# Key-feature sums of layer B through two additions on GpSimd, and a new table of order

## The chip, the cores and the metric

The kernel runs on one core of one Trainium2 chip. The metric is the device time of one execution in microseconds, as the median over several runs. Five engines work side by side, each through its own list of instructions in order: PE (TensorE, matrix products into PSUM), ACT (ScalarE), DVE (VectorE), POOL (GpSimd) and SP (SyncE, which here issues nearly all DMAs). They wait for one another by semaphores only.

## What is computed

Two layers A and B alternate, twice, on 2048 tokens of 512 features with 32 heads of 16. A is attention inside four segments of 512 tokens plus a memory of the earlier segments; B is linear attention whose features are softmaxes over the 16 features of a head. All arrays are bf16. Cut to what matters here:

```python
# A, for each segment s
logits = einsum('bhqd,bhkd->bhqk', qs, ks) * scale + mask
a_dot = einsum('bhqk,bhkd->bhqd', softmax(logits), vs)
a_mem = (phi(qs) @ M) / (phi(qs) @ z + 1e-6)
o = g * a_mem + (1 - g) * a_dot
# B
pk = einsum('bhsd,hdf->bhsf', k, w_phi)
phi_k = concatenate([softmax(pk, -1), softmax(-pk, -1)], -1)
kv = einsum('bhsf,bhsd->bhfd', phi_k, v)
z = einsum('bhsf->bhf', phi_k)
o = einsum('bhqf,bhfd->bhqd', phi_q, kv) / (einsum('bhqf,bhf->bhq', phi_q, z) + 1e-6)
# the block, done twice with the same weights
x = x + A(layernorm(x));  x = x + B(layernorm(x))
```

The softmaxes of B need, for each token, head and sign, the sum over 16 exponentials. These sums over the key features are what the change is about.

## The kernel before

The program first records every operation as a node of a graph, with what it reads, writes and which engines could do it (`Graph.op`, L130; an entry such as `{"dve": (262.0, fn)}` gives the engine, a planned duration in ns and the code). Nothing in the program orders these nodes by itself: `ORDER`, a compressed text at the end of the file, holds one list over all operations, the engine of each, and the buffer of each tile. `place` (L157) reads it, and `emit` (L190) writes each engine's instructions in the order of the list, with a semaphore wait wherever an operand, or a buffer that is used again, comes from another engine. So two things set when an instruction can start: its place in its engine's list, and its waits. The planned durations have no effect on the chip.

Buffers come from pools: `pQ` (6 key-mask tiles), `pK` (6 query tiles), `p1` and `p2` (16 and 19 general tiles of 512 and 1024 bf16 elements, both shown as `p` in the profile), `pE`, `pF` (exponentials of the diagonal blocks), `pT`, `pV`, `pW` (values), `pS` (small f32 tiles), and `pD`, four PSUM tiles of 1024 f32 (shown as `D`).

`setup` (L450) loads the inputs, makes the constants on GpSimd and DVE (identity, head pattern, the triangle `tri` and `two64` that add the mask through a matmul), scales the value weights WA_v by the gates (L530, on GpSimd) and clears parts of the pools.

For each segment, `ln` (L574) does the layer norm: statistics on DVE (L577, L578), the reciprocal root on GpSimd (L585, L587; on ACT for the first four tiles) and the scaling on DVE (L594, L598), then a transposition by DMA (L364) or PE. `a_proj` (L658) projects keys and queries of a group g of 8 heads into one PSUM tile. The keys are copied out by ACT or DVE (`Kev`, by `evac`, L358 to L360), and four masks per group (L679, label `Km`, tile `pQ`) each copy them with all heads but some set to zero, so that one matmul makes the logits of several heads: 4 groups x 4 segments x 2 layers x 4 = 128 instructions of 128x512, all on DVE. `phi` (L629) makes the memory's features (L634, L635).

`a_att` (L768) makes the logits on PE from masks and queries (labels `S`, `Sf`, `Sd`, the matmuls of L326 that read `pQ`), ACT takes the exponential out of PSUM (L351), and PE multiplies with the values (L326, `pV` and `pW`). DVE divides (L846, L847) and adds the memory part (L851). `out_proj` (L877) adds to X (L898 on DVE, or a copy by ACT or DVE where PE adds X itself).

`b_keys` (L922) takes one or two token tiles at a time. PE projects them (`BK`), ACT makes the exponentials of both signs (`kexp`, 1024 elements for two tiles), DVE sums each run of 16 (L945), takes the reciprocal (L389, tile `pT`) and multiplies it into the values straight out of PSUM (L973), and PE multiplies with the exponentials (`KV`, L341 with `pT`); DVE accumulates (L911). Per layer there are seven units of two tiles and two of one, so 28 sums of 1024 elements and 8 of 512 in all. `b_query` (L987) does the queries.

Of the kernel before, what the change touches and what calls it, by code (L numbers as in the profile page):

```python
# [17 lines left out]
H = 32  # L18
# [279 lines left out]
class Kernel:  # L298
# [16 lines left out]
    def sb(self, name, shape, dt):  # L315
        return self.es.enter_context(self.nc.sbuf_tensor(name, shape, dt))
# [79 lines left out]
    def alloc(self):  # L396
# [9 lines left out]
        self.two64 = sb("two64", [128, 2, 64], BF16)  # L406
        self.tri = sb("tri", [128, 64], BF16)
# [42 lines left out]
    def setup(self):  # L450
# [39 lines left out]
        for g in range(NG):  # L490
            for hf in range(2):
# [16 lines left out]
        v(lambda e: e.tensor_tensor(self.two64[:], self.ident[:, 0:64][:, None, :].to_broadcast([128, 2, 64]),  # L508
                                    self.ident[:, 64:128][:, None, :].to_broadcast([128, 2, 64]), ALU.add), 120, [R("ident")], [R("two64")])
        tw = self.T(self.p1, "fold")  # L510
        v(lambda e: e.memset(tw.t[:, 0:128], -1e9), 150, [], [tw], eng=P)
        v(lambda e: e.affine_select(tw.t[:, 0:128], tw.t[:, 0:128], [[-1, 128]], ALU.is_gt, 0.0, base=0, channel_multiplier=1), 250, [tw], [tw], eng=P)
        for hf in range(2):
            v(lambda e, hf=hf: e.tensor_copy(self.tri[64 * hf:64 * hf + 64, :], tw.t[64 * hf:64 * hf + 64, 64 * hf:64 * hf + 64]), 100,
              [tw], [R("tri", hf)])
# [142 lines left out]
    def a_proj(self, L, s):  # L658
# [7 lines left out]
        for g in range(NG):  # L666
# [11 lines left out]
            for sl in range(4):  # L678
                fn = lambda e, KM=KM, KT=KT, sl=sl: e.tensor_scalar(  # L679
                    KM.t[:, :, sl % 2, :, 64 * (sl // 2):64 * (sl // 2) + 64], KT.t[:].rearrange("p (j h k) -> p j h k", j=4, h=2),  # L680
                    self.m4[:, sl:sl + 1], None, op0=ALU.mult)
                self.g.op({"dve": (262.0, fn)}, [KT, R("m4")], [KM[sl]], label="Km", port=True)
# [85 lines left out]
    def a_att(self, L, s, i0):  # L768
# [7 lines left out]
        oT = self.oT[("a", L, s * 4 + i0)] = self.T(self.p2, "oT")  # L776
        two = lambda hf: self.two64[64 * hf:64 * hf + 64].rearrange("p a b -> p (a b)")
        tri = lambda hf, n: self.tri[64 * hf:64 * hf + 64, None, :].to_broadcast([64, n, 64])
        trir = [R("two64"), R("tri", 0), R("tri", 1)]
        for gg in range(2):  # L780
            PV = self.T(self.pD, "pv")
            for g in (2 * gg, 2 * gg + 1):
# [5 lines left out]
                for j in range(i0 + 1):  # L788
                    for p in range(2):
# [6 lines left out]
                        else:  # L796
                            P = PF[p] = self.T(self.pF, "PF")
                            self.mm(lambda S=S, j=j, p=p, key=key, qry=qry: [
                                (S.t[:, hf * 512 + 256 - 192 * x:hf * 512 + 512 - 256 * x], key(hf, j, p, x), qry(hf, 64 * x, 256 - 64 * x), x == 0, False)
                                for x in range(2) for hf in range(2)] + [  # L800
                                (S.t[:, hf * 512 + 64:hf * 512 + 448].rearrange("p (b c) -> p b c", b=2)[:, :, 0:64], two(hf), tri(hf, 2), False, True) for hf in range(2)],
                                [], rd + trir, [S], opens=[P], label="Sf", rows=64, dur=252)
                            self.act(lambda P=P: P.t[:, :, 64:512], lambda S=S: S.t[:].rearrange("p (a b) -> p a b", a=2)[:, :, 64:512], ACT.Exp, 896, [S], [P],
                                     scale=0.25, label="expf")
                S = self.T(self.pD, "S")
                PE = self.T(self.pE, "PE")
                self.mm(lambda S=S, key=key, qry=qry: [
                    (S.t[:, hf * 512 + p * 192 + 64 * (1 - x):hf * 512 + p * 192 + 192 - 128 * x], key(hf, i0 + 1, p, x), qry(hf, 128 + 64 * x, 128 - 64 * x), p + x == 0, False)
                    for p in range(2) for x in range(2) for hf in range(2)] + [
                    (S.t[:, hf * 512:hf * 512 + 384].rearrange("p (a b) -> p a b", a=2)[:, :, 0:128], two(hf), tri(hf, 4), False, True) for hf in range(2)],  # L810
                    [], rd + trir, [S], opens=[PE], label="Sd", rows=64, dur=286)
                self.act(lambda PE=PE: PE.t[:, :, 64:256], lambda S=S: S.t[:, :].rearrange("p (a b) -> p a b", a=2)[:, :, 0:384].rearrange("p a (c e) -> p a c e", c=2),
                         ACT.Exp, 768, [S], [PE], scale=0.25, label="expd")

# [107 lines left out]
    def b_keys(self, L, c, parts):  # L922
# [4 lines left out]
        for part in parts:  # L927
            Es, Vts = {}, {}
            units = [part[i:i + 2] for i in range(0, len(part), 2)]
            for u in units:  # L930
# [9 lines left out]
                for sgn in range(2):  # L940
# [3 lines left out]
                             ACT.Exp, 512 * n, [S[0], S[512]][:n], [E[sgn]], scale=1.0 - 2.0 * sgn, label="kexp")  # L944
                    fn = lambda e, sgn=sgn, eo=eo, Z=Z, n=n: e.tensor_reduce(Z.t[:, 0:64 * n].rearrange("p (k s h) -> p k s h", k=n, s=2)[:, :, sgn, :],  # L945
# [177 lines left out]
COPIED = {(L, t) for L in range(2) for t in range(16)}  # L1123
N_WARM = 26
# [5 lines left out]
c-rlH1GFW}vTa60y4Ggfwr$(CZQHhO+qP}nw(ag$wYu*)=lb4<KmHrz)!wTzvnn%k=8PGUReP@_tTL;@;<M;1F{{d|vFfY_tI2Ay+N=(%%j&WEtO0At8nMQ#32Vxlv  # L1130
F5A=Ysp%%)~pR{%i6K_tOJX~G>gk(u$U|s14ay4QRc9GtQdR3^0PAR5-Y$8vf?ZmE5ypOa;!Wn!5HIAF~NdZWM)}*_LSvdIaw}Nl2u^2*=6>OMPtud0(OO6W$9T)R+
trGrC4%SnpI?ZSYB3%^<y_!3U-qvV)s}=cAvdqx7cm=fIVcHSZbDrrDJJXR+fcjW`<>8ci1)7k@aVt*Z|g<4P|{<5B7+SVv>bncUdqCVUJk^HjoWrgV<o!ouy>)SQj
>$jbUTia2NrT*bFujX0lN*opoj1SWniA&0<SfR4M{RVLn^RIzty&#=61^)(r|lVOYslvEHmF3}egLY&L<-W5ZcAn#20AFOZPNvAOIzd&#0OAKS&&u+=OQ+spQ_P!^W
;0tUGtH)MnC0FVQ6!Yej{4TaYX!GTn4BuhkJ0dN8P$`tru7<7lVY#n>U*0Ub)jeTUvAP?k+d{6-LLP3}a$zc+#fwfQ^N<uLx0sWyb3;+%v7=c0!?;r(~f`zO!B&YZA
mQ7~wSw9#LDPc5hfC(@LQo%+T0%Kt+OoMSSp2cRVAq9PB8`wMci6QoeJ}?;8!6LRE5>pad%m_73VI04~2bjnN8vG6xKf)%M0+V4LPGth7vCU8x2Ej%)AIm{S*u(-LH
aWPN4TR}nU<Q0<)uB8jWpQW=+sPzUg6L2KDnM<RgE62E%*Cou4QfIys0;OA9#nz(&;aT~We8vqSs>fZ%78>4W@DcqCM1G*kQib?LudqzVH+%iee4k14$EN)B!T_xFp
CedVLM9-OJNr5fFPI+J7Ez7!yH%)bD;?=fTpkl_CNyo0Y6v>M27GX1;Rm8hycwXEktFXAsk~E5dt9;62eS4#?rtSwgDHyMqCM7;0RlVTVXZsg<04ZBEeDC9Kt{g2nz
>TJBS7c*&198yJ0r2#hO?Pcfl&y2m2uow1>FV5;{ODNJ;T1E_8&gtTk+7wQ(KR!Sz@an_@Gpgq3jy7Q;5s2@ZgT;<$s&#A_H84`Efjj#cn5R>x>q4I5$&oQ46|2oGQ
&M#ngq0H<RRCd7jn79(OLyZ|k*IX1?N&;$=ceQb#hur9X3dbj`&K{yP-Fc^&SDLlr)nAjTI;9-b?r{D;jhD&e-7UB}@i-mA0_QOTk5ewsDEP|=%3`D215QEM^TRaM#
@CYu$m3RzS;8Dy3Jux#J$766DVq+Fqj=eA)^v3ki8Bah42*s<A2s1)b>VsXdKMuh5*Z~J(cN~P9um^U<E!Yh=<2KxZ=iwv_#vz!R;^I(@NtfX|T!X}TlC{HOSQ3*_8  # L1140
amFl;x0UacVIi7#J#kS?!rBI06TFvX2vUc6|-Pg+=F{D9-hL}I2>=_2#iGuXdmv!5_li-VGbOL1uz>vgqwH<Z@^j1h57Lk-oyKN6Yk(;yo*V2C+(u7m<(^jEl7`%@e
yRioR}L^Vpezz889_oz(@EPZ{ZWTjjL%5J%#7+40h8VdWb9OJf6c&^Z+m7Dr!NUsU^LJ4)g|6;1hg`X)rs!h2)qCCtxa^hy^hUcBJLBf@;!QYDKl^DXpW{^o-I{7wS
ssC=1o5^fU@HP(x}&S*a)Wpk~yLn$rt-Oi$<~bffmPp4w7(+DvUIExv+h*o!h#Z`w#3s19wRP4t}hQ(byN2WT{AqwG|V^58|<PTS}bU0{dl2sNgQY!Xh!DL4kl;to1
WTWKjBqvtpdGtn~2NH6dpy~F`@hz8OrdPv9V1ofkn^oU;JM?6hu=q!E0yx4%oV>&#+reb^?LH(&54WcGAk_OXNDo<nR8jYo<RFx{wI2umna0m^h@>q?kQw1DF<LNRD
qwhGH&eKGiKtJ#bT_8rE@e5X>ulO4K&>MV<?{E@Lri%C;r_gIEOmC?Oy`gu61XPNOQfbOTFX<KKq*lB&|429K1HC7rT$G<~Q32{pQ>i|kqX_s7Kj1XFPB-W_O{Y7Qm
vWP!e3XX@5~mqdh-Ok7-j;u&KKwpCpuW5m_T#1T9;N2}c^ZC~2JtdDpFYzUl9ZVb=2>`Jt|&Wi$J6l~+){g<m1pA)`KSghpyE`9zS1lzOS5SqEh0l@QPUh+Os7~9o|
FgDY4(kl&^eZgXXJC~Jex<kc}kv(=iwdrcS^;(@tiz8&%itKPP{ws%#-mSG=dkS5)?ocsS4%gl_?)j&b#oDd;sst2Xe-Ps3ZYT!GlTh5DMVKcpx9ngLnw<$$Rl0yf<
# [81 lines left out]
```

## Time and profile before

| | |
|---|---|
| median of three runs | 483.2 us (482.02 to 483.73) |
| span of the profiled execution | 481.9 us |
| instructions | 25218 |
| HBM read, written | 6.32 MB, 2.10 MB |
| granted TensorE clock, mean | 0.988 |

The profile is of one execution, and its span runs from the first to the last instruction; the time of a run holds a little more. A row of a group of instructions reads: line of the kernel, engine, operation, output and inputs by tile, shapes, count, then busy time in us and mean duration in ns, then the engine's idle time just before them and what ended it. A busy time counts overlapping stretches once, so it can be below count times mean. "PEld" is PE's loading of weights, which overlaps its matmuls. The chain of waits follows the last instruction back to what released it, step by step.

### The profile page before, as it was taken

To read this page: it belongs to the slowest core of one execution; us is meant where nothing else is said; L and a number is where in the kernel's file an instruction comes from. 1 tells how busy PE (TensorE), PEld (TensorE's weight loads), DVE (VectorE), ACT (ScalarE), POOL (GpSimd) and SP (SyncE) were. 2 spreads that over 40 slices of the span, in tenths; PEclk is the share of its full clock that TensorE was granted. 3 is DMA by queue.
4 is the path that set the end of the run, shared out by engine and by line. 5 is a ranking of instruction groups with operands and counts; after the bars stand their busy time and mean duration, and the time that the engine had idled before them with its cause. 6 is when DMAs were issued, how large, how long until landed. Compare 5 with 4: busy or idle time off the path is not lost.

```text
span 481.9 us, 25218 instructions
## 1 busy us (share of the span) xinstructions
PE 452.9 (94%) x11582; PEld 298.4 (62%) x11582; DVE 438.3 (91%) x920; ACT 425.9 (88%) x560; POOL 63.8 (13%) x145
## 2 busy tenths in 40 slices
PE   8798889999989999998999999999999999999895
PEld 3346665757767677666555677576667666666553
DVE  4998999899889999898999999999999897998883
ACT  2598999999989998578999999999999999776892
POOL 2801120101010110200231041020002020110000
PEclk9999999999999999998999999999999999999799
DMA  8735254350144212200225344432204403100256
GB/s 216 199 83 139 39 90 69 47 86 21 41 68 69 37 15 48 41 1 5 46 52 96 57 72 59 79 67 47 31 4 62 77 16 59 37 12 3 46 93 196
DMA packets 89451, 30.37 MB, mean 63 GB/s; under 512 B 76000, under 2 KB 89344, under 8 KB 89344
## 3 DMA queue, kind: packets, MB, share of 16 engines
q1 hardware_dynamic: 88992, 28.46, 32.1%
q8 instruction: 91, 1.49, 1.3%
q10 hardware_dynamic: 288, 0.26, 0.2%
q0 software_dynamic: 64, 0.02, 0.1%
q14 instruction: 16, 0.13, 0.1%
HBM read 6.32 MB, written 2.10 MB: 17 GB/s over the span
## 4 chain that ended last, share of the span: by engine, by line
PE 54%; DVE 20%; ACT 17%; DMA 3%; issue 2%; SPq 2%; POOL 1%; DVEq 0%
PE D L341 35%; PE D L326 18%; ACT p L351 9%; ACT pF L351 5%; DVE p L635 3%; DVE pQ L679 2%; DVE stats L577 2%; ACT pE L351 2%; SPq L364 2%; DVE p L360 1%; DMA X<-in_A_x_dram 1%; DVE p L598 1%; DVE pK L360 1%; DVE p L847 1%; DMA pX<-p 1%
## 5 line engine op out<-in xcount | busy, mean ns | idle before, releaser
L351 ACT ACTIVATE p<-D 128x1024 bf16<-128x1024 f32 (+1 forms) x276 | 251.5, 956 | 27.5 <-PE D L341 15.9
L351 ACT ACTIVATE pF<-D 128x896 bf16<-128x896 f32 x128 | 117.3, 938 | 2.7 <-PE D L326 2.0
L326 PE MATMUL D<-pK,pQ 64*128 64x256 bf16 (+3 forms) x1536 | 113.9, 243 | 6.1 <-DVE pQ L679 2.3
L326 PEld LDWEIGHTS D<-pK,pQ 64*128 64x128 bf16 x1536 | 54.9, 94 | 45.6 <-ACT p L351 5.8
L326 PE MATMUL D<-pV,pF 64*128 64x34 bf16 x1024 | 75.8, 176 | 1.7 <-ACT pE L351 0.5
L326 PE MATMUL D<-pW,pF 64*128 64x34 bf16 x1024 | 73.0, 176 | 0.5 <-issue 0.5
L585 POOL TENSOR_SCALAR rstd<-mv 128x1 f32<-128x1 f32 x60 | 18.6, 321 | 357.4 <-DVE mv L578 357.4
L341 PE MATMUL D<-pX,WA_k 64*128 64x512 bf16 x256 | 64.7, 376 | 0.7 <-DVE pX L360 0.7
L341 PE MATMUL D<-pX,WA_q 64*128 64x512 bf16 x256 | 64.7, 377 | 0.1
L326 PEld LDWEIGHTS D<-pV,pF 64*128 64x128 bf16 x1024 | 56.8, 93 | 5.3 <-issue 2.2
L326 PEld LDWEIGHTS D<-pW,pF 64*128 64x128 bf16 x1024 | 52.4, 93 | 1.3 <-issue 0.5
L351 ACT ACTIVATE pE<-D 128x768 bf16<-128x768 f32 x64 | 52.5, 830 | 0.8 <-PE D L326 0.4
L326 PE MATMUL D<-pV,p 64*128 64x34 bf16 x1024 | 52.2, 175 | 0.9 <-issue 0.6
L326 PE MATMUL D<-pW,p 64*128 64x34 bf16 x1024 | 51.1, 176 | 0.0
L326 PEld LDWEIGHTS D<-pV,p 64*128 64x128 bf16 x1024 | 46.7, 93 | 2.7 <-ACT p L351 0.5
L326 PE MATMUL D<-tri,two 64*128 64x128 bf16 (+1 forms) x384 | 46.2, 234 | 0.0
L326 PEld LDWEIGHTS D<-pW,p 64*128 64x128 bf16 x1024 | 45.1, 93 | 1.6
L577 DVE BATCH_NORM_STATS2 stats<-X 128x6 f32<-128x512 bf16 x64 | 42.7, 680 | 3.7 <-DMA X<-in_A_x_dram 3.4
L326 PE MATMUL D<-pV,pE 64*128 64x34 bf16 x512 | 45.0, 175 | 0.0
L679 DVE TENSOR_SCALAR pQ<-p,m 128x512 bf16<-128x512 bf16 x128 | 44.2, 366 | 0.1
L326 PE MATMUL D<-pW,pE 64*128 64x34 bf16 x512 | 42.7, 175 | 0.3 <-issue 0.3
L945 DVE TENSOR_REDUCE pS<-p 128x64 f32<-128x1024 bf16 (+1 forms) x36 | 38.6, 1084 | 1.3 <-ACT p L351 1.3
(118 smaller groups left out, 1001.5 us busy)
## 6 DMA issues: line engine op xcount, KB each, us to landing
pW<-pV SPq DMA_DIRECT2D x16, 136.0 KB, 2.8
out_dram<-X SPq DMA_DIRECT2D x7, 256.0 KB, 3.3
X<-in_A_x_dram SPq DMA_DIRECT2D x3, 512.0 KB, 6.4
pX<-in_B_wqkv_dram SPq DMA_DIRECT2D x3, 512.0 KB, 5.2
p<-p SPq DMA_TRANSPOSE x76, 2.6
pX<-p SPq DMA_TRANSPOSE x54, 3.3
WA_k<-in_A_wk_dram SPq DMA_DIRECT2D x2, 256.0 KB, 6.4
WA_q<-in_A_wq_dram SPq DMA_DIRECT2D x2, 256.0 KB, 8.0
```

Of the source, the lines that this page charges most:

```text
L326: ins = e.matmul(out_ap, lhsT, rhs, start=st, stop=sp, tile_position=(basep(lhsT), basep(out_ap)))
L341: ins = e.matmul(out_ap, lhsT[64 * hf:64 * hf + 64], rhs[64 * hf:64 * hf + 64], start=k == 0 and i == 0, stop=k == 1 and i == len(lists[hf ...
L351: return self.g.op({"act": (dur, lambda e: e.activation(out_ap(), in_ap(), func, scale=scale))}, reads, writes, opens, label=label)
L360: "dve": ((340 if fast else n / 0.96 + 65), lambda e: e.tensor_copy(out_ap(), in_ap()))}
L364: return self.g.op({"sp": (1200.0, lambda e: [e.dma_start(out_ap(), in_ap(), transpose=True)])}, reads, writes, opens, kind="d", lat=1450. ...
L577: v(lambda e: e.bn_stats(self.stats[:, t, :], self.X[:, t, :]), 602, [R("X", t)], [R("st", t)], label="bn")
L585: v(lambda e: e.tensor_scalar(rs, self.mv[:, t, 1:2], LN_EPS, None, op0=ALU.add), 170, [R("mv", t)], [R("rstd", t)], eng="pool", label="rstd")
L598: v(lambda e: e.tensor_scalar(xn.t[:], self.X[:, t, :], self.mv[:, t, 0:1], self.rstd[:, t:t + 1], op0=ALU.subtract, op1=ALU.mult), 300, [ ...
L635: v(lambda e: e.scalar_tensor_tensor(dst.t[:], e_.t[:], 1.0, dst.t[:], op0=ALU.min, op1=ALU.add), 335, [dst, e_], [dst], label="phadd", po ...
L679: fn = lambda e, KM=KM, KT=KT, sl=sl: e.tensor_scalar(KM.t[:, :, sl % 2, :, 64 * (sl // 2):64 * (sl // 2) + 64], KT.t[:].rearrange("p (j h ...
L847: v(lambda e, pvv=pvv, rden=rden, part=part: e.tensor_tensor(part(o).rearrange("p (a h d) -> p a h d", a=2, h=16), pvv()[:, :, :, 0:16], r ...
L945: fn = lambda e, sgn=sgn, eo=eo, Z=Z, n=n: e.tensor_reduce(Z.t[:, 0:64 * n].rearrange("p (k s h) -> p k s h", k=n, s=2)[:, :, sgn, :], eo( ...
```

## The change

Four things differ; the last follows from the table alone.

In `b_keys`, the 28 sums of two-tile units (`HALVED` holds all eight pairs of layer and chunk) are made in three steps. GpSimd adds the lower eight of each 16 exponentials to the upper eight into an f32 tile `zs` of `p2` (512 results), adds four to four in place (256 results), and DVE sums the last four. The eight sums of one-tile units stay as they were.

The key masks (L679 before, L689 after) may be done by GpSimd too.

`setup` makes a further constant, `keep`, with two GpSimd memsets, two selects and four DVE copies. It is read only by a way of masking after the exponential (`cut`) that the constants `CUTF` and `CUTD` turn off; with both off the matmuls of the logits are those of before.

```diff
+        big = self.T(self.p1, "fold")
+        for k, top in enumerate((1.0, 3.0e38)):
+            v(lambda e, top=top: e.memset(big.t[:, 0:128], top), 150, [], [big], eng=P)
+            v(lambda e: e.affine_select(big.t[:, 0:128], big.t[:, 0:128], [[1, 128]], ALU.is_ge, 0.0, base=0, channel_multiplier=-1), 250, [big], [big], eng=P)
+            for hf in range(2):
+                v(lambda e, k=k, hf=hf: e.tensor_copy(self.keep[64 * hf:64 * hf + 64, k, :], big.t[64 * hf:64 * hf + 64, 64 * hf:64 * hf + 64]),
+                  150, [big], [R("keep", k, hf)])
...
-                self.g.op({"dve": (262.0, fn)}, [KT, R("m4")], [KM[sl]], label="Km", port=True)
+                self.g.op({"dve": (262.0, fn), "pool": (650.0, fn)}, [KT, R("m4")], [KM[sl]], label="Km", port=True)
...
+                    if (L, c) in HALVED and n == 2:
+                        sc = self.T(self.p2, "zs")
+                        e3 = lambda eo=eo: eo().rearrange("p (k d) -> p k d", d=16)
+                        s3 = lambda sc=sc: sc.t[:].bitcast(F32).rearrange("p (k d) -> p k d", d=8)
+                        self.g.op({"pool": (1120.0, lambda e, e3=e3, s3=s3: e.tensor_tensor(s3(), e3()[:, :, 0:8], e3()[:, :, 8:16], ALU.add))},
+                                  [E[sgn]], [sc], label="zh")
+                        self.g.op({"pool": (600.0, lambda e, s3=s3: e.tensor_tensor(s3()[:, :, 0:4], s3()[:, :, 0:4], s3()[:, :, 4:8], ALU.add))},
+                                  [sc], [sc], label="zh")
+                        fn = lambda e, sgn=sgn, s3=s3, Z=Z, n=n: e.tensor_reduce(Z.t[:, 0:64 * n].rearrange("p (k s h) -> p k s h", k=n, s=2)[:, :, sgn, :],
+                                                                                s3().rearrange("p (k h) d -> p k h d", k=n)[:, :, :, 0:4], AX.X, ALU.add)
+                        v(fn, 332, [sc], [Z[sgn]], label="Zred4")
+                        continue
...
+CUTF, CUTD = False, False
+HALVED = {(L, c) for L in range(2) for c in range(4)}
```

The new table keeps the rough course of the old one, and moves instructions and engines within it. Counted in the lists of the two built programs:

| | before | after |
|---|---|---|
| PE matmuls | the same | the same, in another order |
| key masks on DVE, GpSimd | 128, 0 | 44, 84 |
| WA_v products on DVE, GpSimd | 0, 4 | 2, 2 |
| additions of the sums on GpSimd | 0 | 56 |
| copies out of PSUM and of weights (`evac`) on ACT, DVE | 38, 87 | 31, 94 |
| DMAs | the same | the same, in another order |

Of the copies, thirteen go from ACT to DVE (twelve of 512 elements, one of 1024) and six from DVE to ACT (five of 512, one of 1024). In the list of loads, both 128-token tiles of X that SP loads now stand ahead of the first tile of 512 tokens, and two loads of WA_o stand ahead of the first of WA_k.

More of the change, by code (lines that the diff above doesn't have):

```diff
@@ L405, in alloc @@
         self.eps6 = sb("eps6", [128, 1], F32)
-        self.two64 = sb("two64", [128, 2, 64], BF16)
-        self.tri = sb("tri", [128, 64], BF16)
+        self.keep = sb("keep", [128, 2, 64], BF16)
+        if not CUTD:
+            self.two64 = sb("two64", [128, 2, 64], BF16)
+            self.tri = sb("tri", [128, 64], BF16)
         self.ones8 = sb("ones8", [128, 8], F32)
@@ L1134 @@
[L1134 to L1145, printed above, removed]
@@ L1191 @@
+cgDV><YA(4Tjl`Thas+x7uPaA2@g7V1k3=d=mq;W=V3d>RU81@q;ee_8Mm+)eG{agbvKBhL|%`IF!OIv?P$3x8cFFEqr-OPA9AGDZ%1M`)jRf9c_1eZRRv;bM=$%12jU
+9G&3-{^t;0(w#d&(!UL6{&{?^ST~qi7j_4szsEi0Ai={B-$vOD6`od(q@fUs5H4Xb%xTmt+*U+S3GM<D=A@K$^(`<wCCK=E^o{VD>^?!^5PVx%+>`=MD1|r{81#GMs~k
+Qpfe=c5*GWh;uB0)S9^nO@v@fgOAb(VR2>a@v7a*KjPAt@Q2D!PUo6{Hkz+is{6IUc$0kjY*nGHriv<fgJ44qL-fJ>lI&<0&)2@YV=)kOz~YoW^l-|Wg&?m$femO?$Wf
+s$jea18hV=ZGty%9VZNQe9H0qkN#R2)oDs1w+C2(f
 """
```

154 lines of the change are left out of this document (88 added, 66 removed).

## The prediction

> **What bounds the kernel now.** First the page's head and its chain of waits:
>
> ```profile
> span 481.9 us, 25218 instructions
> PE 452.9 (94%) x11582; PEld 298.4 (62%) x11582; DVE 438.3 (91%) x920; ACT 425.9 (88%) x560; POOL 63.8 (13%) x145
> PE 54%; DVE 20%; ACT 17%; DMA 3%; issue 2%; SPq 2%; POOL 1%; DVEq 0%
> ```
>
> No single engine is the answer: three are near 90% of the span, and the chain changes hands between them. So I split the span at the places where the mix changes, which the view by stages gives (busy time of PE, PEld, DVE, ACT and POOL after the length of each stretch):
>
> ```profile
> 0.00:24.00 24.00, 19.18 (x184) 9.06 (x186) 17.54 (x46) 9.82 (x22) 13.07 (x33) 1.00 0.79 208
> 24.00:168.00 144.00, 135.15 (x3744) 91.87 (x3740) 134.50 (x286) 137.61 (x176) 16.33 (x36) 1.00 0.37 66
> 168.00:216.00 48.00, 47.75 (x1196) 33.35 (x1192) 44.67 (x77) 38.96 (x46) 4.92 (x12) 1.00 0.17 26
> 216.00:240.00 24.00, 21.60 (x587) 13.81 (x582) 20.54 (x52) 21.57 (x35) 3.20 (x8) 0.93 0.12 24
> 240.00:408.00 168.00, 162.98 (x4507) 110.35 (x4508) 160.12 (x349) 165.27 (x213) 23.14 (x48) 1.00 0.36 56
> 408.00:456.00 48.00, 45.80 (x1023) 28.87 (x1016) 44.31 (x85) 35.77 (x50) 3.17 (x8) 0.93 0.11 22
> 456.00:482.00 26.00, 20.42 (x372) 11.08 (x368) 16.61 (x31) 16.87 (x25) 0.00 (x0) 0.97 0.58 139
> ```
>
> In the two attention stretches (24 to 168 and 240 to 408) ACT is the fullest engine: it is idle 144 - 137.6 = 6.4 us in the first and 168 - 165.3 = 2.7 us in the second, while DVE is idle 9.5 and 7.9. From 168 to 216 PE is full (0.25 us idle). DVE is full nowhere. So time taken off DVE isn't time taken off the span: it can only win back what ACT and PE lose to DVE's lateness, and let DVE take work from ACT.
>
> **What is removed, and what it costs on DVE.** The rows by shape for the instructions that leave or move:
>
> ```profile
> L945 DVE TENSOR_REDUCE pS<-p 128x64 f32<-128x1024 bf16 x28 | 33.4, 1206 | 1.3 <-ACT p L351 1.3
> L945 DVE TENSOR_REDUCE pS<-p 128x32 f32<-128x512 bf16 x8 | 5.2, 658 | 0.0
> L679 DVE TENSOR_SCALAR pQ<-p,m 128x512 bf16<-128x512 bf16 x128 | 44.2, 366 | 0.1
> L635 DVE SCALAR_TENSOR_TENSOR p<-p 128x512 bf16<-128x512 bf16 x48 | 32.0, 674 | 0.2
> L514 DVE COPY tri<-p 64x64 bf16<-64x64 bf16 x2 | 0.3, 166 | 0.0
> L360 DVE CAST p<-D 128x512 bf16<-128x512 f32 x27 | 18.5, 684 | 1.9 <-PE D L867 1.4 <-PE D L341 0.4
> L360 DVE CAST pV<-D 128x1024 bf16<-128x1024 f32 x13 | 15.9, 1223 | 2.2 <-PE D L341 2.1
> L360 DVE COPY pX<-D 128x512 bf16<-128x512 bf16 x4 | 1.7, 420 | 0.5 <-PE D L378 0.5
> L359 ACT ACTIVATE p<-D 128x512 bf16<-128x512 f32 x15 | 9.1, 608 | 5.7 <-PE D L341 5.4 <-PE D L867 0.4
> L359 ACT ACTIVATE X<-D 128x1024 bf16<-128x1024 f32 x5 | 5.3, 1051 | 0.0
> ```
>
> The 28 long sums now read 256 elements. The trace has no such sum; its two lengths give (1206 - 658) / 512 = 1.07 ns an element, so 658 - 256 x 1.07 = 384 ns. Saved: 28 x 0.82 = 23.0 us.
>
> The larger part isn't in the change's name. The new table puts 84 of the 128 key masks of L679 on GpSimd: 84 x 44.2/128 (345 ns of busy time each) = 29.0 us less on DVE. It also swaps copies out of PSUM. Twelve of 512 elements and one of 1024 go from ACT to DVE, five and one come back: ACT -7 x 0.608 = -4.3 us; DVE +4 x 0.42 + 8 x 0.684 - 5 x 0.684 = +3.7 us (the two long ones cancel). New on DVE are two of the four WA_v products (as L635, 0.67 each), four copies for the unused `keep` (0.17 each) and a small memset: +2.2 us. DVE: 438.3 - 23.0 - 29.0 + 3.7 + 2.2 = 392.2 us, 81% of the span, before it waits for anything new.
>
> **What it costs on GpSimd.** The nearest rows:
>
> ```profile
> L530 POOL TENSOR_TENSOR WA_v<-WA_v,gt 128x512 bf16<-128x512 bf16 x4 | 4.3, 1110 | 0.0
> L587 POOL TENSOR_TENSOR rstd<-rstd,mhalf 128x1 f32<-128x1 f32 x60 | 36.4, 619 | 2.6
> L506 POOL TENSOR_SCALAR_AFFINE_SELECT ident<-ident 128x128 bf16<-128x128 bf16 x1 | 0.3, 310 | 0.1
> L499 POOL TENSOR_SCALAR_AFFINE_SELECT H<-ones 128x8 f32<-128x8 f32 x1 | 0.2, 202 | 0.0
> ```
>
> The first addition has two inputs and 512 results, as L530: 1.11 us. The second has 256 results: between L587's 0.62 (one element, but a power) and 1.11; I take 0.62, since half of L530 is 0.56. A mask has one input; the selects grow by 108 ns over 120 elements, so 512 would take 0.202 + 504 x 0.0009 = 0.66 us; the ends are 0.31 and 1.11. New load: 28 x 1.73 + 84 x 0.66 = 48.4 + 55.4 = 104 us, which makes GpSimd about 167 us (35%): no bound. What counts is its latency. Each sum becomes available two additions later (1.73 us), and behind it on DVE wait the reciprocal L389, the products L973 and then PE's L341 products of pT. And GpSimd runs its list in order: behind an addition that waits for ACT's exponential stand the variance roots L585/L587 and the next masks, and for the masks waits PE.
>
> **What the two engines do to each other.** The trace has one place where GpSimd ran long instructions beside DVE's masks, one where DVE ran long ones beside GpSimd, and the spread of GpSimd's shortest instruction:
>
> ```profile
> 16.35 4.33 POOL L530 TENSOR_TENSOR WA_v<-WA_v,gt 128x512 bf16<-128x512 bf16 x4
> 17.08 4.31 DVE L679 TENSOR_SCALAR pQ<-p,m 128x512 bf16<-128x512 bf16 x5
> 21.16 0.39 PE L326 MATMUL D<-pK,pQ 64*128 64x256 bf16 x4 [2.26 <-DVE pQ L679]
> 244.14 1.44 POOL L585 TENSOR_SCALAR rstd<-mv 128x1 f32<-128x1 f32 x1 [4.14 <-DVE mv L578]
> 244.14 0.68 DVE L1043 TENSOR_TENSOR p<-p,pS 128x1024 bf16<-128x1024 bf16 x1
> L585 POOL TENSOR_SCALAR rstd<-mv x60: 202/221/1439, 11.1 to 424.0; 128x1 f32<-128x1 f32 x60
> L585 POOL TENSOR_SCALAR rstd<-mv 128x1 f32<-128x1 f32 x60 | 18.6, 321 | 357.4 <-DVE mv L578 357.4
> ```
>
> Five masks took 4.31 us instead of 5 x 0.345 = 1.73, one per GpSimd instruction, and PE stood 2.26 us. In the other direction a 0.22 us instruction took 1.44. So each engine can hold the other for an instruction. In the list of the changed program 55 of the 140 new GpSimd instructions have, within their own length, a DVE instruction of the kinds that read two SBUF tensors or are masks, copies and scalings from SBUF. If the first such one waits half the GpSimd instruction (0.33 us for 37 masks, 0.43 on average for 18 additions), DVE loses 12 + 8 = 20 us; the ends are nothing and the full length of all 140, 104 us. With 20, DVE stands at 412 us (86%), still 26 below now.
>
> The Trainium skill, SBUF — State Buffer, section "Who interferes with whom", says that the two share a port pair as an exclusive lock, so that the later one blocks fully, and that a DVE instruction with at most one SBUF input outside the two-port modes is free of it; the rows at 17.08 and 244.14 agree, and by that rule the short sums, which have one input, would hold nobody.
>
> **The sum.** The span of the profiled execution is 481.9, and the runs' median of 483.2 lies 1.3 above it; I add that back.
> - ACT's own load from 240 to 408, where it is idle 2.7 us only: six short copies leave and a long one comes, -6 x 0.608 + 1.051 = -2.6 us on the engine that ends last there. From 24 to 168 the swaps cancel: 0.
> - Waits of ACT that DVE causes: ACT's idle time in both stretches is 9.1 us (ends 0 and 9.1). DVE holds 20% of the chain, so I take 20%: -1.8.
> - New waits for masks: eleven of the 32 groups of masks now have the last mask directly ahead of the first PE block that reads it in the table's list (one before), ten of them on GpSimd. Each costs at least what GpSimd's short instruction loses on average, 321 - 221 = 0.10 us: +1.1.
> - From 168 to 240 and after 408 PE has the same matmuls: 0. At the start, two WA_v products on DVE and two on GpSimd still alternate with the first masks, and the two small X tiles load ahead of the large one but two WA_o loads ahead of WA_k: 0, with 1 us to either side.
>
> -2.6 - 1.8 + 1.1 = -3.3: span 478.6, time 479.9.
>
> **The rivals.**
> - A (above), 479.9; own range 476 (half of ACT's 9.1 us idle gone, no new wait: -7.2) to 481.7.
> - B, the relief is hidden: ACT and PE stay as full, since DVE was idle 17 us in the attention stretches already, and the copies' 2.6 us go to new waits: 483. Against it stands that ACT's load does fall.
> - C, slower by just-in-time masks: the median group had 13 PE blocks between its last mask and its first reader and now has 2. If two masks of a group on GpSimd are each held by one 0.67 us DVE instruction (L635 stands beside the masks in each projection), PE gets that group 1.35 us late, ten times 13.5 us; less A's gains of 4.4 that is +9.1, 492.3. If the exponential in work on ACT (0.94 us, the row below) covers most of each, 10 x 0.41 cancels the gains: 483. I take the middle, 487.7. It decides from 0.44 us a group on.
>
> ```profile
> L351 ACT ACTIVATE pF<-D 128x896 bf16<-128x896 f32 x128 | 117.3, 938 | 2.7 <-PE D L326 2.0
> ```
>
> - D, the lock eats the relief: DVE held for the full length of most of the 104 us of new GpSimd work, as at 17.08. At 85% DVE has 392 + 88 = 480 us of work, and its idle time at both ends (6.5 in the first 24 us, 9.4 in the last 26) makes 496. It decides above three quarters (392 + 78 + 16 = 486). For it: the row at 17.08 shows just this; against it: many of DVE's instructions read PSUM.
>
> The Trainium skill, Perfetto Trace Analysis, section "Optimizing Scalar/DVE Operations", warns that moving work from DVE to GpSimd might not help because of the shared port; that is D, and the trace shows it at 17.08 only.
>
> **How the numbers follow.** A 0.47, B 0.13, C 0.31, D 0.09. A measurement of this kernel tells some 0.3% (1.45 us) from no change, so faster is A, 0.47; same is B, 0.13; slower is C and D, 0.40. The range goes from 475 (A's best and a start that gains its 1 us) to 489.5 (C's middle with 1.8 above it), leaving out D and C's upper third, about 0.17, and little below. A's own range stands above.
>
> **What would show it.** The rows of before for DVE's other scalings from SBUF:
>
> ```profile
> L598 DVE TENSOR_SCALAR p<-X,mv,rstd 128x512 bf16<-128x512 bf16 x48 | 18.8, 402 | 1.4 <-POOL rstd L587 1.2
> L634 DVE TENSOR_SCALAR p<-p 128x512 bf16<-128x512 bf16 x24 | 6.7, 281 | 0.0
> ```
>
> Right: the short sums near 0.38 us, masks on GpSimd near 0.66, first additions near 1.1; DVE's busy time near 412; ACT from 240 to 408 shorter by about 2.6 us and still idle under 3. C: waits of PE's L326 weight loads or matmuls on GpSimd's masks, several us in all, and ACT idle more in the attention stretches. D: the mean of DVE's L598, L634, L635 and of the remaining masks well above 402, 281, 674 and 345 ns, and DVE's busy time at 440 or more. Wrong altogether: masks on GpSimd at 1.1 us or more, which would double C's price, or a start that shifts by more than 1 us.

## The result, and the profile after

The changed kernel takes 516.7 us (516.06 to 517.38, four runs) against 483.5 us for the kernel before in the same comparison: the ratio is 1.070, with an interval of 1.066 to 1.074. The forecast was 479.9 us in a range of 475 to 489.5. It is outside, and on the other side of no change. Some executions run slower at a lower clock (489.4 us at 0.938, where the kernel before otherwise takes some 483); the times and ratios below leave them out.

The head of the page after, and its chain of waits by engine:

```profile
span 514.3 us, 25309 instructions
PE 465.0 (90%) x11582; PEld 303.5 (59%) x11582; DVE 425.8 (83%) x850; ACT 428.0 (83%) x553; POOL 246.0 (48%) x286
PE 50%; DVE 16%; POOL 16%; ACT 13%; DMA 3%; issue 2%; POOLq 0%; DVEq 0%
```

Every engine has a smaller share than before except GpSimd (on the chain 16% now, 1% before), and the span is 32.4 us longer: nothing became full, the engines wait for one another. PE's idle time went from 481.9 - 452.9 = 29.0 to 514.3 - 465.0 = 49.3 us, 20.3 more. The other 12.1 us are PE's busy time, for the same matmuls. The two attention stretches show where the time goes (granted clock third from the end). The rows are cut so that they hold about the matmuls of the rows before: 3742 against 3744, and 4422 against 4507.

```profile
24.00:184.00 160.00, 142.16 (x3742) 94.58 (x3740) 130.72 (x247) 138.59 (x176) 96.70 (x98) 0.96 0.35 59
260.00:436.00 176.00, 162.54 (x4422) 108.70 (x4416) 152.86 (x304) 161.53 (x204) 101.90 (x105) 0.99 0.32 51
```

The first stretch takes 160 us where it took 144, about half of the loss. The clock was 1.00 in both before. ACT, idle 6.4 and 2.7 us in these stretches before, is now idle 21.4 and 14.5. The view of waits says what came new (releaser, us in total, times, longest); first three rows of the kernel before, then the changed kernel:

```profile
ACT p L351 <- PE D L326: 8.5, 11, 2.1
PEld D L326 <- DVE pQ L679: 3.0, 2, 2.8
PE D L326 <- DVE pQ L679: 2.3, 1, 2.3
```

```profile
POOL p L973 <- ACT p L351: 66.0, 13, 16.5
POOL pQ L689 <- DVE p L360: 34.4, 10, 10.6
ACT p L351 <- PE D L326: 22.3, 27, 3.3
PEld D L326 <- POOL pQ L689: 15.6, 8, 3.7
PE D L326 <- POOL pQ L689: 12.5, 7, 3.6
```

PE's weight loads now wait for masks on GpSimd eight times and its matmuls seven, and ACT waits for PE's logits. The matmuls' waits for masks rose from 2.3 to 12.5 us, half of the 20.3 us by which PE stands idle longer. The rows of GpSimd's new work, and of two of DVE's instructions named in the prediction:

```profile
L689 POOL TENSOR_SCALAR pQ<-p,m 128x512 bf16<-128x512 bf16 x84 | 135.9, 1628 | 45.3 <-DVE p L360 34.4 <-ACT p L359 8.9 <-DVE mv L588 1.9
L973 POOL TENSOR_TENSOR p<-p 128x512 f32<-128x512 bf16 x28 | 32.3, 1157 | 68.6 <-ACT p L351 66.0 <-DVE pS L977 2.7
L975 POOL TENSOR_TENSOR p<-p 128x256 f32<-128x256 f32 x28 | 21.4, 772 | 1.2
L977 DVE TENSOR_REDUCE pS<-p 128x64 f32<-128x256 f32 x28 | 11.1, 408 | 9.0 <-POOL p L975 8.9
L608 DVE TENSOR_SCALAR p<-X,mv,rstd 128x512 bf16<-128x512 bf16 x48 | 22.6, 480 | 4.0 <-ACT rstd L593 2.0 <-POOL rstd L597 1.7
L689 DVE TENSOR_SCALAR pQ<-p,m 128x512 bf16<-128x512 bf16 x44 | 19.2, 445 | 0.0
L689 POOL TENSOR_SCALAR pQ<-p,m x84: 1557/1580/2069, 16.7 to 418.2; 128x512 bf16<-128x512 bf16 x84
```

A mask takes 1.58 us (the median of the last row) where 0.66 was forecast. The longest wait of the matmuls, seen on GpSimd in order of time:

```profile
154.91 2.27 POOL L973 TENSOR_TENSOR p<-p 128x512 f32<-128x512 bf16 x2 [4.91 <-ACT p L351]
157.26 1.48 POOL L975 TENSOR_TENSOR p<-p 128x256 f32<-128x256 f32 x2
158.76 9.46 POOL L689 TENSOR_SCALAR pQ<-p,m 128x512 bf16<-128x512 bf16 x6
```

GpSimd stands 4.9 us at an addition whose exponential isn't there, then does 3.75 us of additions, then six masks back to back. PE's readers of `pQ` stood still 3.6 us in that stretch.

### The profile page after: what moved, and what is told of

It reads as the page before. It is cut to its first block, busy times and chain, and to the rows that moved or that the text cites. A ratio compares the mean times of both kernels' runs of the same rounds, so it can differ in the third digit from the quotient of the medians.

```text
span 514.3 us, 25309 instructions
## 1 busy us (share of the span) xinstructions
PE 465.0 (90%) x11582; PEld 303.5 (59%) x11582; DVE 425.8 (83%) x850; ACT 428.0 (83%) x553; POOL 246.0 (48%) x286
## 4 chain that ended last, share of the span: by engine, by line
PE 50%; DVE 16%; POOL 16%; ACT 13%; DMA 3%; issue 2%; POOLq 0%; DVEq 0%
PE D L341 33%; PE D L326 16%; POOL pQ L689 11%; ACT p L351 7%; ACT pF L351 4%; DVE stats L587 2%; DMA pX<-p 2%; POOL rstd L597 2%; DVE p L360 2%; DMA beta_sb<-in_A_beta_dram 1%; ACT pE L351 1%; POOL p L973 1%; DVE p L645 1%; DVE p L644 1%; DVE p L608 1%
## 5 line engine op out<-in xcount | busy, mean ns | idle before, releaser
L351 ACT ACTIVATE p<-D 128x1024 bf16<-128x1024 f32 (+1 forms) x276 | 252.1, 949 | 45.6 <-PE D L326 22.3
L689 POOL TENSOR_SCALAR pQ<-p,m 128x512 bf16<-128x512 bf16 x84 | 135.9, 1628 | 45.3 <-DVE p L360 34.4
L326 PE MATMUL D<-pK,pQ 64*128 64x256 bf16 (+3 forms) x1536 | 115.9, 247 | 21.0 <-POOL pQ L689 12.5
L351 ACT ACTIVATE pF<-D 128x896 bf16<-128x896 f32 x128 | 116.1, 932 | 9.0 <-PE D L326 8.2
L326 PEld LDWEIGHTS D<-pK,pQ 64*128 64x128 bf16 x1536 | 54.9, 95 | 59.8 <-POOL pQ L689 15.6
L341 PE MATMUL D<-pX,WA_k 64*128 64x512 bf16 x256 | 66.7, 385 | 0.9 <-DMA pX<-p 0.3
L341 PE MATMUL D<-pX,WA_q 64*128 64x512 bf16 x256 | 66.7, 385 | 0.1
L973 POOL TENSOR_TENSOR p<-p 128x512 f32<-128x512 bf16 x28 | 32.3, 1157 | 68.6 <-ACT p L351 66.0
L595 POOL TENSOR_SCALAR rstd<-mv 128x1 f32<-128x1 f32 x60 | 15.1, 256 | 91.3 <-DVE mv L588 91.1
L326 PE MATMUL D<-pV,p 64*128 64x34 bf16 x1024 | 53.6, 177 | 0.8 <-DVE X L922 0.5
L326 PE MATMUL D<-pW,p 64*128 64x34 bf16 x1024 | 52.5, 177 | 0.0
L326 PEld LDWEIGHTS D<-pV,p 64*128 64x128 bf16 x1024 | 47.8, 94 | 4.6 <-DVE X L922 0.8
```

What stands on the lines that cost most here:

```text
L326: ins = e.matmul(out_ap, lhsT, rhs, start=st, stop=sp, tile_position=(basep(lhsT), basep(out_ap)))
L341: ins = e.matmul(out_ap, lhsT[64 * hf:64 * hf + 64], rhs[64 * hf:64 * hf + 64], start=k == 0 and i == 0, stop=k == 1 and i == len(lists[hf ...
L351: return self.g.op({"act": (dur, lambda e: e.activation(out_ap(), in_ap(), func, scale=scale))}, reads, writes, opens, label=label)
L595: v(lambda e: e.tensor_scalar(rs, self.mv[:, t, 1:2], LN_EPS, None, op0=ALU.add), 170, [R("mv", t)], [R("rstd", t)], eng="pool", label="rstd")
L689: fn = lambda e, KM=KM, KT=KT, sl=sl: e.tensor_scalar(KM.t[:, :, sl % 2, :, 64 * (sl // 2):64 * (sl // 2) + 64], KT.t[:].rearrange("p (j h ...
L973: self.g.op({"pool": (1120.0, lambda e, e3=e3, s3=s3: e.tensor_tensor(s3(), e3()[:, :, 0:8], e3()[:, :, 8:16], ALU.add))}, [E[sgn]], [sc], ...
```

## The experiments

Eighteen kernels ran. The kernel before took 482.3 to 483.5 us in the five comparisons, and ratios are against the runs of the same one.

### Is relief of VectorE worth anything?

e11 leaves the kernel before as it is, but sums 4 terms instead of 16.

```diff
-  eo().rearrange("p (k h d) -> p k h d", k=n, h=H), AX.X, ALU.add)
+  eo().rearrange("p (k h d) -> p k h d", k=n, h=H)[:, :, :, 0:4], AX.X, ALU.add)
```

> The kernel before with its 36 long sums taken over the first 4 of their 16 terms, on VectorE at the same places; the sums over the other 12 terms are left out. VectorE is relieved of 28 times 0.8 us and 8 times 0.4, 25 us, with nothing put on GpSimd and no wait added. Theory 'VectorE's load hardly sets the time': 480 to 483 us, as the prediction's 20 per cent of a small idle time has it. Rival 'VectorE bounds': 470 us or less.

```profile
PE 451.9 (94%) x11582; PEld 298.6 (62%) x11582; DVE 414.5 (87%) x920; ACT 425.5 (89%) x560; POOL 64.0 (13%) x145
```

484.6 us, ratio 1.002 (0.999 to 1.005). DVE lost 23.8 us of work and the time did not move. In this order the named purpose of the change has nothing to win; that a new order, which fills the room on DVE with ACT's copies, has nothing to win either is not shown by it.

### Why does a mask take 1.58 us?

e4 sets 13 forms of GpSimd instruction behind the kernel before, alone; some of them:

```diff
+        do(lambda e, i: e.tensor_scalar(km(i), vj(a), m[:, i:i + 1], None, op0=ALU.mult))
+        do(lambda e, i: e.tensor_scalar(cn(i)[:, 0:512], a[:], m[:, i:i + 1], None, op0=ALU.mult))
+        do(lambda e, i: e.tensor_scalar(cn(i)[:, 0:512], a[:], 2.0, None, op0=ALU.mult))
...
+        do(lambda e, i: e.tensor_copy(cn(i)[:, 0:512], a[:]))
```

> The kernel before with 52 instructions more on GpSimd behind its last additions, four of each of 13 forms, one after the other with nothing else running; only their durations are read, the time of the whole says nothing. Theory 'a mask costs what it costs': the mask's form (512 columns of bf16 times one number per partition, written in strides) takes 1.5 to 1.6 us alone, the same to a contiguous target within 0.1 us of it, and the same with a constant in place of the number per partition shows whether that number is the price. Rival 'the mask is slowed by its neighbours': alone it takes 0.6 to 1.1 us, and the 1.58 us of the changed kernel come from the lock shared with VectorE. Half the columns (256) should take half of the part that goes with columns; 64 columns show the fixed part.

The groups by line: the mask's form (L1079), contiguous (L1080), with a constant (L1081), 256 and 64 columns, two inputs, a copy:

```profile
L1079 POOL TENSOR_SCALAR pQ<-p,m 128x512 bf16<-128x512 bf16 x4 | 6.3, 1572 | 0.4
L1080 POOL TENSOR_SCALAR pQ<-p,m 128x512 bf16<-128x512 bf16 x4 | 6.2, 1562 | 0.4
L1081 POOL TENSOR_SCALAR pQ<-p 128x512 bf16<-128x512 bf16 x4 | 5.9, 1487 | 0.3
L1083 POOL TENSOR_SCALAR pQ<-p,m 128x256 bf16<-128x256 bf16 x4 | 3.7, 922 | 0.4
L1084 POOL TENSOR_SCALAR pQ<-p,m 128x64 bf16<-128x64 bf16 x4 | 1.8, 442 | 0.4
L1086 POOL TENSOR_TENSOR pQ<-p 128x512 bf16<-128x512 bf16 x4 | 4.6, 1149 | 0.3
L1087 POOL COPY pQ<-p 128x512 bf16<-128x512 bf16 x4 | 2.4, 612 | 0.3
```

The price is the instruction's own: neither the strides, nor the number per partition (75 ns against a constant), nor a neighbour makes it. It is (1572 - 922) / 256 = 2.54 ns a column and some 0.27 us beside. A product of two tensors is quicker (1.15) than a product with a number (1.57). The Trainium skill, GPSIMD Engine Reference, section "Engine selection", calls one-input work on GpSimd roughly line-rate and two-input work some 2 times slower than VectorE; here the one-input mask is the slower of the two and 4.6 times VectorE's 0.345 us.

### The two halves alone, in the old order

e8 moves the change's 84 masks to GpSimd and nothing else; e5 begins the 28 long sums there and nothing else, each pair of additions right behind its exponential in the list, with a buffer that is idle by the list, and the short sum just ahead of its reciprocal.

```diff
+        for o, f in zip([o for o in self.ops if o.label == "Km"], ON_POOL):
+            o.eng = "pool" if f == "1" else "dve"
```

> The kernel before, its own table and its own long sums, with the same 84 masks moved to GpSimd at the places where VectorE had them. Theory 'a mask on GpSimd does no harm where it has cover': the cover is 5 us and more in 16 of 32 groups and under 3.5 us in 13, so only the latter wait: 478 to 490 us. Rival 'GpSimd itself': 84 masks of 1.58 us (133 us) in GpSimd's order, with the variance roots behind them and VectorE's copies slowed by 20 us: 495 us or more.

513.1 us, 1.060 (1.051 to 1.069).

> The kernel before with its own table, all masks on DVE, and only the 28 long sums changed: two additions on GpSimd right behind the exponential, the short sum on DVE moved to directly ahead of the reciprocal that needs it, the sums' tile in buffers that stand empty there. Late masks: the sums alone take 28 x (1206 - 408) ns = 22 us off DVE and cost PE nothing, so 478 to 484 us. Rival, the sums' latency and the lock cost: 488 or more.

516.5 us, 1.068 (1.062 to 1.073). Each half costs as much as the whole. In e8 GpSimd's masks make PE and the roots' readers wait:

```profile
PEld D L328 <- POOL pQ L681: 18.6, 5, 6.9
PE D L328 <- POOL pQ L681: 16.5, 5, 6.4
DVE nb L594 <- POOL rstd L589: 13.3, 5, 7.6
```

In e5 there are no masks on GpSimd, and the waits show the head of the queue; first GpSimd, then DVE in order of time:

```profile
143.44 1.15 POOL L987 TENSOR_TENSOR p<-p 128x512 f32<-128x512 bf16 x1 [16.45 <-ACT p L388]
...
145.37 0.22 POOL L622 TENSOR_SCALAR rstd<-mv 128x1 f32<-128x1 f32 x1
```

```profile
146.28 0.41 DVE L635 TENSOR_SCALAR p<-X,mv,rstd 128x512 bf16<-128x512 bf16 x1 [6.29 <-POOL rstd L624]
```

An addition stood 16.4 us for an exponential; behind it stood a variance root of 0.22 us, and DVE stood 6.3 us for that. DVE waited for roots 20.0 us in all, against some 1.4 before.

### The same halves, placed so that nothing urgent stands behind them

e10 moves 22 of the 28 sums and e13 even 97 of the 128 masks, each to a place chosen by the times in the profile before: its input ready, no root due while it runs, and its reader 0.7 us or more later.

```diff
+        for z1, z2, z4, sc, (k1, k4, name, slot) in self.new:
+            z1.seq, z2.seq, z4.seq, z1.eng, z2.eng = k1, k1 + 0.0005, k4, "pool", "pool"
```

> The kernel before with 22 of its 28 long sums begun on GpSimd, as in the earlier run that did it for all 28 (516.5 us), but each pair of additions is put where, by the times of the profile before, the exponential and the borrowed buffer have been done for 0.25 us, no variance root becomes due within the 2 us that they take, and VectorE's short sum comes 0.7 us or more behind them. Theory 'the additions cost by standing at the head of GpSimd's queue': without that the loss of 33 us goes, 478 to 488 us, and VectorE's wait for the roots goes from 20 us back to some 2. Rival 'the additions cost by the lock and by their latency to the reciprocal': 500 us or more.

491.5 us, 1.014 (1.010 to 1.019), above the 478 to 488 that was expected; DVE's wait for roots is down from 20.0 us to 2.5:

```profile
DVE p L616 <- POOL rstd L605: 2.5, 5, 1.1
```

> The kernel before, its own long sums on VectorE, with 97 of its 128 masks moved to GpSimd, more than the change moves: each goes where, by the times of the profile before, the key copy and the buffer have been done for 0.25 us, no variance root becomes due within its 1.65 us, no other mask is on GpSimd, and 0.7 us or more are left to the first reader. The same 84 masks as in the change, at VectorE's old places in the order, took 513.1 us. Theory 'place, not engine': 480 to 490 us, and the weight loads' wait for masks goes from 18.6 us back to some 3. Rival 'masks on GpSimd cost by their 1.6 us and by the lock': 500 us or more.

490.6 us, 1.016 (1.010 to 1.021): more masks on GpSimd than in e8, and 22 us less.

```profile
L685 POOL TENSOR_SCALAR pQ<-p,m 128x512 bf16<-128x512 bf16 x97 | 158.4, 1647 | 41.5 <-DVE p L366 24.0 <-ACT p L365 17.5
PE D L332 <- POOL pQ L685: 8.0, 1, 8.0
```

GpSimd carries 158 us of masks, and PE waits for one of them once, 8.0 us, where the kernel before waits 2.3 us for a mask on DVE. Its first matmuls that read `pQ` begin at 26.0 us, in the kernel before at 21.2; GpSimd around that, in order of time:

```profile
15.46 4.72 POOL L536 TENSOR_TENSOR WA_v<-WA_v,gt 128x512 bf16<-128x512 bf16 x4
...
21.84 8.71 POOL L685 TENSOR_SCALAR pQ<-p,m 128x512 bf16<-128x512 bf16 x5
```

Five masks stand behind the products of the value weights and other work of the start, which the rules of the placing leave out. So the place made some three quarters of both losses: 25 of 33 us for the sums (of which the six left on DVE may be 7, by their share) and 22 of 30 for the masks. Place means two things here that these runs don't separate, what stands behind an instruction and how long before its reader it is done. The remaining 8 or 9 us hold what the engine itself costs, with its 1.6 us a mask and the lock (each engine holding up the other), and what is still ill placed.

### The new table without the work on GpSimd

e1 does all masks on DVE at the new table's places, e2 all long sums in one step, e3 both.

```diff
+            if o.label == "Km":
+                o.eng = "dve"
```

> The changed kernel with all 128 key masks on DVE again, at the same places of the list; sums and table as changed. Late masks (a mask on GpSimd takes 1.58 us instead of the 0.66 assumed, and PE waits for it): 480 to 490 us, DVE's busy time near 426 + 84 x 0.345 - 20 (held less) = 435, and no wait of PE on masks over 3 us in all. Rival, the sums' two additions late and GpSimd's list blocked behind them: over 500. Rival, the new table itself is worse: over 500.

518.0 us, 1.071 (1.069 to 1.073).

> The changed kernel with the 28 long sums made by DVE in one step again (no additions on GpSimd); the 84 masks stay on GpSimd, table as changed. Late masks: 508 to 518 us, with masks still 1.58 us and PE still waiting for them. Rival, sums: 480 to 490. Rival, the table: over 505 too, and then e3 tells it from the masks.

518.8 us, 1.073 (1.070 to 1.075).

> Masks and sums both on DVE, with the new table: what is left is the new order, the seven copies moved on balance to DVE and the unused constant. Late masks or sums: 481 to 490 us. The table itself worse: over 500.

524.7 us, 1.084 (1.081 to 1.088). With masks of 0.35 us on DVE the time is that of 1.58 us on GpSimd, and with nothing left of the work on GpSimd it is worst. So the table is dear without any of it. Its places were made with that work on GpSimd, though, so that the 41 us of e3 are no share of the changed kernel's 33. e1's waits for masks, now from DVE, are longer in total than after:

```profile
PEld D L328 <- DVE pQ L691: 23.5, 13, 3.6
PE D L328 <- DVE pQ L691: 18.9, 11, 3.1
```

### Late masks

e9 takes the kernel before and puts its masks, all on DVE, directly ahead of their readers (or of the next user of the key copy's buffer); e6 and e7 take the new table and put them forward, on DVE and on the change's engines; e12 is e6 with the long sums in one step.

```diff
+            o.seq = max(o.was, min(first, end) - 0.5)          # e9
+            o.seq = min(o.was, max(max(d.seq for d in o.deps) + 14.0, free + 6.0))     # e6, e7, e12
```

> The kernel before with its own engines throughout; in its order only the masks move back, to directly ahead of the group's first reader, or of the next user of the key copy's buffer where that is sooner. 20 of 32 groups then have no PE work between the last mask and the reader (before 1, changed table 12). Theory 'late masks are dear by themselves': rival C's 2.0 us of PE wait a third of the groups would give some 10 to 20 us: 493 to 503 us. Rival 'VectorE runs ahead of its readers, so a late place is hidden': 483 to 488 us, and the loss of the changed table lies elsewhere.

548.1 us, 1.134 (1.129 to 1.138): 65 us from nothing but the place of 128 instructions in one engine's list.

```profile
PEld D L342 <- DVE pQ L695: 43.9, 15, 4.9
PE D L342 <- DVE pQ L695: 38.3, 15, 4.4
```

> The changed kernel with all 128 masks on VectorE and in the written order up to 30 places earlier: each stands 14 places behind its key copy, or 6 behind the last user of its buffer, where that is earlier than the table has it. The PE work that the list puts between a group's last mask and its first reader is then 11 us or more for most groups (the changed table has 0 to 2 us for half of them, the table before 5). Theory 'late masks': with the cover back, most of the loss goes: 485 to 500 us, and the waits of the weight loads for a mask (15.6 us after) fall below 4 us. Rival 'the rest of the table, and the sums': the masks' waits go, and others take their place: 510 to 520 us, as with the masks on VectorE at the late places (518).

509.5 us, 1.055 (1.049 to 1.060).

> The changed kernel with its own engines for the masks (84 on GpSimd) and only their places in the order moved forward, as in the run above. Theory 'late masks': 485 to 500 us, as above, since 4 masks of 1.58 us are 6.3 us and most groups now have 11 us or more of cover. Rival 'the rest of the table, and the sums': 510 to 520 us, though the weight loads wait for masks less than 4 us. Third theory 'GpSimd's queue': masks at 1.58 us that stand earlier push the variance roots and the first additions back on GpSimd, and the time comes out above the 516.7 us of the changed kernel.

530.2 us, 1.099 (1.093 to 1.106).

> The changed table with nothing of the change left on GpSimd: the long sums in one step on VectorE at the short sums' places, all masks on VectorE, 14 places behind their key copy. With the masks late this was 524.7 us; with the masks early and the sums begun on GpSimd it was 509.5 us. Theory 'the table loses by its order on the other engines': 505 to 515 us. Rival 'in this table too the sums on GpSimd are the rest of the loss': 490 us or less.

514.8 us, 1.066 (1.063 to 1.069). On DVE the earlier place wins back 8.5 us (e1 to e6) and 9.9 (e3 to e12), a part of the loss and not most of it. On GpSimd it costs 13.5 us more: the third theory of e7. There the masks push back what stands behind them, and DVE waits for roots 20.6 us (two rows of the same view):

```profile
DVE p L623 <- POOL rstd L612: 11.6, 6, 5.0
DVE nb L617 <- POOL rstd L612: 9.0, 5, 4.1
```

### GpSimd's order alone, in the changed kernel

e17 keeps every engine and every order but GpSimd's, whose 282 operations move by 3 places in the mean. The places were chosen by working the lists through with the durations of the rows after.

> The changed kernel, every operation on its own engine, with its own order on all engines but GpSimd; GpSimd's 282 operations (masks, additions, variance roots) are moved by 3 places in the mean, chosen with the durations that the profile after shows (mask 1.58 us, additions 1.16 and 0.77). Theory 'part of the 33 us is GpSimd's queue, ordered for masks of 0.65 us': 500 to 508 us. Rival 'only the late places against the readers count, and VectorE's order': 513 us or more.

505.6 us, 1.048 (1.043 to 1.054): at least 11 us of the 33 are the order that the table gives GpSimd (the program plans 0.65 us a mask). PE's waits for masks fell from 15.6 and 12.5 us to 6.4 and 5.3:

```profile
PEld D L326 <- POOL pQ L689: 6.4, 3, 2.7
PE D L326 <- POOL pQ L689: 5.3, 3, 2.2
```

### VectorE's order: four runs that did not separate it

e14 and e15 exchange VectorE's whole order between the tables; e16 (on the table without GpSimd work) and e18 (on the changed kernel) work it over by single moves. Only the table differs in each, and in e16 to e18 one line that says when a buffer counts as taken.

> The kernel before, all its operations on its own engines, with its own buffers and its own order on TensorE, ScalarE, GpSimd and the DMA queue; only VectorE's order is that of the changed table (masks and sums on VectorE at the places where that table has them; an operation that would stand ahead of what it needs is put back behind it). Theory 'VectorE's order in the new table is the loss': 515 to 530 us, as with the new table whole and all the work on VectorE (524.7). Rival 'the loss lies in the order of the other engines or in the buffers': 483 to 495 us.

689.3 us, 1.428 (1.419 to 1.436).

> The reverse of the run above: the changed table's buffers and its order on TensorE, ScalarE, GpSimd and the DMA queue, long sums and masks on VectorE, and VectorE's order that of the kernel before. Theory 'VectorE's order is the loss': 483 to 492 us. Rival 'the order of the other engines or the buffers': 505 to 525 us, near the 514.8 us of the run with the masks alone put forward.

652.3 us, 1.352 (1.345 to 1.359). Both ways are far worse than either table: VectorE's list of one table does not fit the other lists of the other table, so the exchange says nothing of which one holds the loss.

> The changed table's buffers and its order on TensorE, ScalarE, GpSimd and the DMA queue, long sums and masks on VectorE in one step (524.7 us in the table's own order), and VectorE's order worked over alone, by moves of single operations, 6 places in the mean, chosen with the durations of the profiles. Theory 'the loss of the table without GpSimd work is VectorE's order': 482 to 495 us. Rival 'the order of the other engines and the buffers keep part of it': 505 us or more.

531.6 us, 1.101 (1.097 to 1.106).

> As the run above, with VectorE's order worked over too (5 places in the mean); ScalarE, TensorE, the DMA queue and the buffers as in the changed table. Theory 'order, not engines': 486 to 500 us, most of the 33 us back and nothing gained on the kernel before, since VectorE's relief alone was worth nothing. Rival 'the work on GpSimd itself costs (1.58 us a mask, the lock)': 505 us or more.

533.4 and 540.5 us, 1.113 (1.102 to 1.124). Both kernels are worse than what they began from. In e16 PE waits for activations transposed by DMA (1.5 and 1.6 us before), so the moves bring a loss of their own and say nothing of what a better order would give:

```profile
PE D L341 <- DMA pX<-p: 13.9, 8, 4.6
PEld D L341 <- DMA pX<-p: 10.7, 7, 2.7
```

So it stays open in part where the 32 us of e12 lie, with its masks early and nothing on GpSimd. Its chain of waits by engine is this:

```profile
DVE 44%; PE 38%; ACT 14%; issue 2%; DMA 1%; POOL 0%; DVEq 0%; POOLq 0%
```

DVE had 20% before. The rows of the view of waits add up to 29.8 us in which e12's matmuls wait for results of DVE, against 9.4 before. That is all of the 20.5 us by which PE stands idle longer, and masks are 1.9 of the 29.8. So other results of DVE come late. Whether its order, its 10.8 us more of work (449.1 against 438.3) or late inputs of its own make them late, no run shows. No version beat the kernel before.

## Why the prediction was wrong

**The sum's frame failed.** It priced the new table by what it adds to each engine and took its order as free: one term, "new waits for masks", ten groups at 0.10 us, +1.1 us. That term is the step that fell. Measured, PE's weight loads waited 15.6 us for masks (3.0 before) and its matmuls 12.5 (2.3 before). The view that shows it was read: the median group's cover falling from 13 PE blocks to 2, rival C. e9 shows the mechanism by itself at 65 us, e3 that the table costs 41 us with none of the new work on GpSimd. The masks are half of PE's new idle time. e17 shows that at least 11 of the 33 us come of GpSimd's order, in part through the same waits; the cause of the rest stays open.

**Rival C had the sign and a piece of the cause,** and three things made it too small. Its masks were 0.66 us, worked out from selects at 0.9 ns a column; the mask's own slope is 2.54. The prediction named 1.1 us or more as the sign that it is wrong altogether, and 1.58 came. Its cover was one exponential, where waits of up to 3.7 us came. And it looked at masks alone. "Behind an addition that waits for ACT's exponential stand the variance roots and the next masks" stands in the prediction as a sentence with no price; e5 and e10 make it up to 25 us in the old order, where DVE waited 20 us for roots. In the changed kernel it waited for roots made on GpSimd 3 us only, and the masks are what stands behind the additions; there e17 finds 11 us in GpSimd's order. These parts overlap and don't add up: the halves alone cost 30 and 33, both together with the new table 33.

**The relief came on the engines and not in the time.** ACT has seven copies fewer, and its rows by shape add up to 468.5 us before and 461.9 after (its busy time, in which overlap counts once, is 425.9 and 428.0). The forecast's -2.6 and -1.8 us did not come of it, since ACT waited more (for the logits 22.3 us instead of 8.5). e11 sets the value of 24 us of DVE's time at nil in the old order, as the opening argument had it (DVE is full nowhere) and as rival B has it.

**The small prices were near.** The short sum is 408 ns (384), the first addition 1.157 us (1.11), the second 0.772 (0.62). GpSimd's busy time is 246 us against 167, and 84 x 0.92 = 77 us of the difference are the masks.

**The lock was about right in size.** The five rows that the prediction named or that read two SBUF tensors (L608, L644, L645, L689 and L875 after) took 16.3 us more than their counts at the durations before; 20 was forecast. Their means grew, which is one of rival D's two signs; the other, 440 us of busy time, did not come (425.8), and neither did the 88 us that D needed. What the 16.3 us cost in time no run separates. That DVE is at 425.8 us and not at 412 is another matter: the prediction took the times of rows off a busy time in which overlapping stretches count once. The rows add up to 24.6 us less (490.1 to 465.5), near the 26.1 of the prediction's terms, but the overlap of the instructions fell too, from 51.8 to 39.7 us.

## What to carry to other kernels

Where instructions are issued in a written order, price a change by the order: for each instruction on a slow or idle engine, what stands behind it, and who waits for that. An engine that is 13% busy is free in time but not in its queue, when others wait for its few short instructions (in e5 and e7, variance roots of 0.2 us). Before moving work off an engine, measure what the relief alone is worth by shortening that work in place; here one run says nil, for the old order. And take the duration of a moved instruction from its own form on its new engine: neighbours in kind were off by a factor of 2.4.

## What the runs showed of the hardware

A wait of PE costs more than itself. The granted clock fell from 0.988 to 0.969 in the changed kernel and to 0.935 in e9, and the same 256 matmuls took 376 (before), 385 (after) and 401 ns (e9) in the mean:

```profile
L341 PE MATMUL D<-pX,WA_k 64*128 64x512 bf16 x256 | 64.7, 376 | 0.7 <-DVE pX L360 0.7
```

```profile
L341 PE MATMUL D<-pX,WA_k 64*128 64x512 bf16 x256 | 66.7, 385 | 0.9 <-DMA pX<-p 0.3 <-ACT p L351 0.3
```

```profile
L357 PE MATMUL D<-pX,WA_k 64*128 64x512 bf16 x256 | 70.1, 401 | 0.7 <-DVE pX L376 0.7
```

The clock fell about as much as the matmuls grew (0.988/0.969 = 1.020 and 385/376 = 1.024; 0.988/0.935 = 1.057 and 401/376 = 1.066). By it alone PE's 452.9 us would become 452.9 x 0.988/0.969 = 461.8, an estimate: 8.9 of the 12.1 us of new busy time.

Cut into stretches of 0.5 and 1 us, the trace after shows when the clock falls. Four single waits of the matmuls, of 2.2 us (at 42.3), 1.7 (at 51.0), 1.9 (at 77.3) and 3.6 (at 164.7), were each followed by a granted clock of 0.50 for some 3.5 us. In such a time PE does some 1.7 us of work less, an estimate, so that a wait of 2 us can cost about twice its length. The Trainium skill, TensorE: Matmul & The Clock Gate, section "HAM oscillation — how this bites in real kernels", puts the gate's limit at idle gaps of about 3.4 us. This trace differs, since the clock fell after the three shorter waits too; no run here shows the limit itself.
